# Token and key scores as eight-tile products, landmark rows on the partitions, landmark matrices 512 columns wide

## The chip, the cores and the metric

The kernel runs on one NeuronCore of a Trainium2 chip. TensorE multiplies matrices, VectorE, ScalarE and GpSimd work on elements, and SyncE issues the transfers. The metric is the device time of one execution in microseconds; the kernel before took 730.0 us (median of three runs, 729.05 to 730.16). In the profile TensorE is PE (its weight loads PEld), VectorE is DVE, ScalarE is ACT, GpSimd is POOL and SyncE is SP.

## The reference

Three layers in fp32: attention through landmarks, a gated MLP, and an MLP with a Mish activation. Four batches, eight heads, 576 tokens, head width 64, 32 landmarks of 18 tokens each.

```python
q_lm = q.reshape(B, H, 32, 18, D).mean(axis=3)
k_lm = k.reshape(B, H, 32, 18, D).mean(axis=3)
A  = sm(q, k_lm)         # token scores: softmax over the 32 landmarks, 576 x 32
Bm = sm(q_lm, k_lm)      # 32 x 32
C  = sm(q_lm, k)         # key scores: softmax over the 576 keys, 32 x 576
Z = Bm.T / (norm1(Bm) * norminf(Bm) + 1e-6)
for _ in range(6):
    Z = 2 * Z - Z @ Bm @ Z
attn = A @ Z @ C @ v                      # heads joined to x, 2304 x 512
x = ((x @ w1) * (x @ w2)) @ w3 @ w_out    # gated MLP, inner width 1024
h = x @ w_in                              # Mish MLP, inner width 2048
out = (h * tanh(softplus(h))) @ w_out2
```

sm(a, b) is the softmax of a @ b.T / 8 over the last axis.

## The kernel before

Everything after the softmaxes is linear up to the product a * b, so the kernel never forms attn. For each batch b it makes L = Z C v (kept transposed, LT, 256 landmark rows of all heads by 64) and from it the landmark matrices M = L w1 and L w2, one block of 128 columns of each (a slice s of eight) at a time. Then a = A M1 and b = A M2 (steps `xa` and `xb`), their product (`xm`) is the hidden h, and h times w3 @ w_out (made ahead by the steps `mm`) is the input y of the last layer (steps `y`). The Mish MLP follows with Strassen products (steps Z, O and their sums).

Products marked fp32 in the listing (scores, `mm`, M) run as two passes each and show as two matmuls in the profile. Products of split operands (high part and rest) run as three matmuls, lines 196 to 198.

Attention of one batch (function `attn`): `qs`, `ks` sum q and k over the 18 tokens of each landmark on DVE (L397). `bdq`, `bdk` place the sums of two heads in block-diagonal tiles (ACT or POOL, `blocks`). `as0` to `as2` make the token scores with tokens on the partitions: for 32 tokens at a time the stationary side is a block of q (128 rows, 32 columns) and the moving side one block-diagonal tile of 64 columns (L426). `amx`, `asb`, `aex`, `asm`, `aad`, `arc`, `amul` are the softmax over runs of 32 columns, in pieces of 512, 512 and (on 64 partitions) 256 columns; `atr` turns the result by PE transposes (L483), and `ahi`, `alo` split it into the tile AT. `cs0`, `cs1` make the key scores (L505, 288 columns, 64 stationary columns), `bs` the landmark scores (L588); `ctr`, `cv`, `lt` lead to LT, and `bp`, `nm`, `nu` are the iteration for Z. `m b s` makes one slice of M: eight fp32 products of 256 columns (L810) on eight tiles of the array, 64 rows by 32 columns each, into two PSUM banks, where each bank takes tiles of both row halves. `mh` (ACT) and `ml` (DVE, L225) split M into a slot of three, which `xa` and `xb` read.

Weights come as 512 KB tiles (`ld`), of which `da` (ACT or DVE) and `db` (DVE, L216) put the fp32 words together.

The order on all engines is written out in the table ORDER; `issue` runs the steps in that order, and each engine then works its instructions off in its own order, waiting for others by semaphores. The eight PSUM banks (pool `w`) are handed out in the same order. So an engine whose next instruction waits holds everything behind it.

Of the kernel before, what the change touches and what calls it, by code (L numbers as in the profile page):

```python
# [1481 lines left out]
```

## Time and profile before

| what | value |
|---|---|
| median of three runs | 730.0 us (729.05 to 730.16) |
| profiled execution | 729.66 us |
| its span, first to last instruction | 727.9 us |
| PE busy | 714.0 us, 98% |
| DVE busy | 410.2 us, 56% |
| ACT busy | 292.3 us, 40% |
| POOL busy | 15.2 us, 2% |
| mean granted PE clock, of full speed | 0.995 |

Shares are means over stages that differ. A line of a view that groups instructions gives their number, their busy time together (time in which at least one of them ran) and the mean duration of one; where matmuls run side by side or overlap, the busy time is far below number times duration. A line of the chain gives the start, the time and what ran.

### The profile page before, as it was taken

Reading aid. Unit: us, or ns where it says so; the run is one execution under the profiler, and the core shown is the slowest. Engines: PE = TensorE matmul, PEld = TensorE weight load, DVE = VectorE, ACT = ScalarE, POOL = GpSimd, SP = SyncE. Lnnn points to the kernel's source line nnn. Section 1 sums busy time; section 2 is a strip of 40 time slices with the busy share of each in tenths; the row PEclk is TensorE's granted clock in tenths of the full one; section 3 lists DMA queues with packets and bytes.
Section 4 is the critical chain, followed back from the end, with each engine's and each line's share of the span. In section 5 each row is a group of like instructions: output and inputs, shape, how many; then the busy total and the mean of one; then the engine's idle time right before and its main releaser. Section 6 shows DMA issues by size and latency. Waiting matters only on the chain.

```text
span 727.9 us, 13793 instructions
## 1 busy us (share of the span) xinstructions
PE 714.0 (98%) x5652; PEld 615.2 (85%) x5652; DVE 410.2 (56%) x896; ACT 292.3 (40%) x673; POOL 15.2 (2%) x37
## 2 busy tenths in 40 slices
PE   7799999999999999999999999999999999999997
PEld 4455899854999999999898898898898998898996
DVE  7889779846744734587565577733323553322322
ACT  2544446424534433465644445633222443222222
POOL 2111000000000000000000000000000000000000
PEclk9999999999999999999999999999999999999999
DMA  9876775343313053526554596687455545455402
GB/s 328 299 275 235 264 232 194 123 146 128 135 59 145 31 203 126 193 100 234 217 217 158 218 386 258 258 299 260 171 209 218 197 190 215 170 206 213 178 1 86
DMA packets 33918, 141.46 MB, mean 194 GB/s; under 512 B 3392, under 2 KB 3776, under 8 KB 30272
## 3 DMA queue, kind: packets, MB, share of 16 engines
q1 hardware_dynamic: 33712, 140.46, 52.4%
q8 instruction: 44, 0.72, 0.4%
q14 instruction: 18, 0.15, 0.1%
q10 hardware_dynamic: 144, 0.13, 0.1%
HBM read 110.69 MB, written 29.88 MB: 193 GB/s over the span
## 4 chain that ended last, share of the span: by engine, by line
PE 95%; DVE 2%; DMA 1%; issue 1%; ACT 0%; SPq 0%; ACTq 0%
PE ps L196 27%; PE ps L198 27%; PE ps L197 27%; PE ps L346 8%; PE ps L810 2%; PE ps L623 1%; DMA k<-in_kT_dram 1%; PE ps L564 1%; PE ps L505 1%; PE ps L483 1%; PE ps L426 1%; DVE sumk L397 1%; PE ps L543 1%; DVE sumq L397 0%; DVE mx L435 0%
## 5 line engine op out<-in xcount | busy, mean ns | idle before, releaser
L196 PE MATMUL ps<-hs,W 128*128 128x288 f32 (+1 forms) x298 | 92.5, 310 | 0.0
L197 PE MATMUL ps<-hs,W 128*128 128x288 f32 (+1 forms) x298 | 92.3, 310 | 0.0
L198 PE MATMUL ps<-hs,W 128*128 128x288 f32 (+1 forms) x298 | 92.2, 309 | 0.0
L1277 DVE TENSOR_TENSOR hsb<-ps,zt 128x384 f32<-128x384 f32 x72 | 39.8, 556 | 91.6 <-PE ps L198 91.6
L196 PE MATMUL ps<-AT,M 128*128 128x288 f32 x256 | 77.7, 303 | 0.0
L1273 ACT ACTIVATE hsb<-hsb 128x768 f32<-128x768 f32 (+1 forms) x48 | 32.8, 684 | 107.7 <-DVE hsb L1277 107.7
L198 PE MATMUL ps<-AT,M 128*128 128x288 f32 x256 | 75.5, 295 | 0.3 <-DVE M L225 0.3
L197 PE MATMUL ps<-AT,M 128*128 128x288 f32 x256 | 75.4, 294 | 0.0
L1277 DVE TENSOR_TENSOR zt<-ps,zt 128x384 f32<-128x384 f32 x48 | 26.7, 556 | 78.5 <-PE ps L198 74.6
L225 DVE TENSOR_TENSOR W<-hsb,W 128x384 fp32r<-128x384 f32 (+1 forms) x72 | 49.2, 686 | 18.1 <-ACT W L1274 18.1
L346 PE MATMUL ps<-wo,raw 128*128 128x512 f32 x128 | 59.4, 607 | 0.0
L196 PEld LDWEIGHTS ps<-hs,W 128*128 128x128 f32 x298 | 56.0, 188 | 2.1 <-issue 0.8
L198 PEld LDWEIGHTS ps<-hs,W 128*128 128x128 f32 x298 | 55.9, 188 | 1.8
L197 PEld LDWEIGHTS ps<-hs,W 128*128 128x128 f32 x298 | 56.1, 188 | 1.3
L196 PEld LDWEIGHTS ps<-AT,M 128*128 128x128 f32 x256 | 48.0, 188 | 3.4 <-issue 1.5
L197 PEld LDWEIGHTS ps<-AT,M 128*128 128x128 f32 x256 | 48.1, 188 | 0.5 <-issue 0.5
L198 PEld LDWEIGHTS ps<-AT,M 128*128 128x128 f32 x256 | 48.0, 188 | 0.5 <-DVE M L225 0.5
L220 ACT ACTIVATE a<-ps 128x288 f32<-128x288 f32 x64 | 25.5, 409 | 56.5 <-PE ps L198 49.9
L346 PEld LDWEIGHTS ps<-wo,raw 128*128 128x128 f32 x128 | 24.2, 199 | 24.9 <-issue 22.2
L204 ACT ACTIVATE top<-raw 128x512 f16<-128x512 bf16 x51 | 39.1, 786 | 14.7 <-DMA raw<-in_wts_dram 9.9
L848 DVE TENSOR_TENSOR h<-a,ps 128x288 f32<-128x288 f32 x64 | 27.9, 448 | 27.4 <-PE ps L198 24.8
L197 PE MATMUL ps<-yH,hs 128*128 128x384 f32 x120 | 40.2, 335 | 0.0
(191 smaller groups left out, 1597.6 us busy)
## 6 DMA issues: line engine op xcount, KB each, us to landing
raw<-in_wts_dram SPq DMA_DIRECT2D x88, 512.0 KB, 4.5
zw<-zd SPq DMA_DIRECT2D x8, 1792.0 KB, 7.5
hs<-zd SPq DMA_DIRECT2D x8, 1792.0 KB, 7.2
zd<-zw SPq DMA_DIRECT2D x4, 1792.0 KB, 7.1
zd<-hs SPq DMA_DIRECT2D x4, 1792.0 KB, 9.7
wy<-wod SPq DMA_DIRECT2D x12, 512.0 KB, 7.9
W<-wod SPq DMA_DIRECT2D x10, 512.0 KB, 7.3
q<-in_qT_dram SPq DMA_DIRECT2D x8, 576.0 KB, 7.5
```

The lines of the kernel that those rows point to most:

```text
L196: T.matmul(out=o, lhsT=lh, rhs=rh, start=first, stop=False, skip_group_check=partial)
L197: T.matmul(out=o, lhsT=lh, rhs=rl, start=False, stop=False, skip_group_check=partial)
L198: T.matmul(out=o, lhsT=ll, rhs=rh, start=False, stop=last, skip_group_check=partial)
L204: S.activation(o, i, ACTF.Copy)
L220: S.activation(o, x, ACTF.Copy)
L225: (G if e == "POOL" else V).tensor_tensor(o, x, f32(hi), op=ALU.subtract)
L346: T.matmul(out=got(f"acc{i}"), lhsT=f32(middle(got(f"w3{n}"))[:, o:o + 128]), rhs=WO0[j // 4][:, j % 4], start=j == 0, stop=j == 7)
L397: V.tensor_reduce(st["s" + x][:, r, :].rearrange("p a l -> p (a l)"), st[x][:, r, :].rearrange("p a (l t) -> p (a l) t", t=BLK_T), axis=AX ...
L810: T.matmul(out=got(f"p{c}{key}")[32 * i:32 * i + 32, 0:256], lhsT=LT[r, b, 2 * c + par, :], rhs=w12(f"w{bp}{s}{c}")[r, par * 256:par * 256 ...
L848: V.tensor_tensor(hslice(u, s), got("s" + key), got("b" + key)[:, 0:HALF], op=ALU.mult)
L1273: S.activation(e, src_, ACTF.Mish)
L1277: V.tensor_tensor(o, x, y, op=ALU.add)
```

## The change

It does these things:

- Token scores: the stationary side is now a landmark sum (64 rows of one head by 32 landmarks), the moving side 288 columns of q. Eight such products, four heads of each group g on 32 partitions each, go to eight tiles of the array (function `scores`). A batch needs two steps of eight products for the tokens (`as0`, `as1`, one for each half of the tokens) and two for the keys (`cs0`, `cs1`). The block-diagonal tiles and their copies go.
- Since softmax over landmarks now runs across partitions, DVE turns each 128x288 piece in blocks of 32x32 straight from PSUM (`at`), the softmax runs on two pieces of 576 columns, and a second block transpose of 576 columns on DVE (`atr`) takes the place of the PE transposes.
- The scale 1/8/18 moves into the exponentials. The landmark scores go to two banks, with one maximum and one subtraction for each.
- M is made for two slices at once: eight products of 512 columns into two full banks; `mt` hands out the slots of M apart from the product, so that a slot is claimed before the split and not before the product. The weight tiles of w1 and w2 are cut to match.
- ORDER is written anew from the first row to the last.

```diff
+        def lm_rows(g, i):
+            p, h2 = 2 * g + i // 2, (i ^ g) % 2
+            return p, slice(64 * h2, 64 * h2 + 64), (64 * h2, 32 * i)
+
+        def scores(key, lm, x, hf):
+            for i in range(4):
+                for g in range(2):
+                    p, r, at_ = lm_rows(g, i)
+                    T.matmul(out=mine(f"{key}{g}{hf}")[32 * i:32 * i + 32, 0:HALF], lhsT=st[lm][r, p, :],
+                             rhs=st[x][r, p, hf * HALF:(hf + 1) * HALF], start=True, stop=True, tile_position=at_)
...
-                            T.matmul(out=sc[r:r + 32, i, p * 64:p * 64 + 64], lhsT=st["q"][:, p, t0 + r:t0 + r + 32],
-                                     rhs=bdk[:, p, :], start=True, stop=True, tile_position=(0, r))
...
+        def a_turn(hf, g):
+            def f(e):
+                st["e", g] = mine(f"e{g}")
+                V.transpose(st["e", g][:, hf * HALF:(hf + 1) * HALF], mine(f"sc{g}{hf}")[:, 0:HALF])
             return f
...
-                        T.transpose(out=tp[:, c, i * 128:i * 128 + w],
-                                    in_=st["e", g][0:w, i, c * 128:(c + 1) * 128], identity=idn[0:w, 0:w])
...
+        def a_back(g):
+            def f(e):
+                V.transpose(mine(f"ea{g}"), st["e", g])
+            return f
...
-                        T.matmul(out=mine(f"cs{g}{hf}")[64 * pr:64 * pr + 64, 0:HALF], lhsT=bdq[:, 2 * g + pr, :],
-                                 rhs=st["k"][:, 2 * g + pr, hf * HALF:(hf + 1) * HALF], start=True, stop=True)
...
+        for hf in range(2):
+            add(f"as{hf}", "PE", [ks, "lq1"], a_scores(hf), (), {f"sc{g}{hf}": "w" for g in range(2)})
+        for hf in range(2):
+            for g in range(2):
+                add(f"at{hf}{g}", "DVE", [f"as{hf}"] + [f"at0{g}"] * hf, a_turn(hf, g), (), {} if hf else {f"e{g}": "e"}, [f"sc{g}{hf}"])
...
-            add(f"atr{g}", "PE", [f"amul{g}"], a_tr(g), (), {f"tp{g}": "w"}, [f"e{g}"])
+            add(f"atr{g}", "DVE", [f"amul{g}"], a_back(g), (), {f"ea{g}": "ea"}, [f"e{g}"])
...
-                    T.matmul(out=got(f"p{c}{key}")[32 * i:32 * i + 32, 0:256], lhsT=LT[r, b, 2 * c + par, :],
-                             rhs=w12(f"w{bp}{s}{c}")[r, par * 256:par * 256 + 256], start=True, stop=True,
+                    T.matmul(out=got(f"p{c}{key}")[32 * i:32 * i + 32], lhsT=LT[r, b, 2 * c + par, :],
+                             rhs=w12(f"w{bp}{s}{2 * c + par}")[r], start=True, stop=True,
                              tile_position=(64 * (h % 2), 32 * i))
...
+        for x in range(2):
+            n = f"{b} {2 * s + x}"
+            step(f"mt {n}", "none", vacated, lambda e: None, {f"M {n}": "M"})
+            for c in range(2):
+                step(f"mh{c} {n}", "ACT", [key, f"mt {n}"], ev(0, c, x))
+                step(f"ml{c} {n}", "DVE", [f"mh{c} {n}"], ev(1, c, x), (), [f"p{c}{key}"])
```

On DVE, at the token softmax of the first batch, the order was this (mx is the maximum, e the scores less the maximum, ps a PSUM bank):

```order
L435 TENSOR_REDUCE mx<-ps_80 128x16
L604 TENSOR_REDUCE bsm<-be 128x2
L397 TENSOR_REDUCE sumq<-q_71 128x64
L607 TENSOR_SCALAR bsm<-bsm 128x2
L514 TENSOR_REDUCE cmx<-ps_83 128x1
L442 TENSOR_TENSOR e_93<-ps_80,mx 128x512
```

It is now this, with the block transposes of batch 0 as they come from PSUM:

```order
L578 TENSOR_REDUCE bsm<-be 128x2
L420 STREAM_TRANSPOSE e_93<-ps_84 128x288
L498 TENSOR_SCALAR csm<-csm 128x1
L393 TENSOR_REDUCE sumk<-k_72 128x64
L581 TENSOR_SCALAR bsm<-bsm 128x2
L584 RECIPROCAL bsm<-bsm 128x2
L503 RECIPROCAL csm<-csm 128x1
L420 STREAM_TRANSPOSE e_94<-ps_83 128x288
L420 STREAM_TRANSPOSE e_94<-ps_77 128x288
```

The transposes stand where the first maximum stood; the first maximum now comes 24 rows behind the first transpose, and reads SBUF.

On PE, from the last product of LT to the first product of `xa` (AT and M are its operands, wo and raw those of an `mm` product, w and LT those of M), the order was this:

```order
L689 MATMUL ps_81<-py,cv 64x32 x2
L810 MATMUL ps_82<-w_875,LT 32x256
L810 MATMUL ps_78<-w_875,LT 32x256
...
L810 MATMUL ps_84<-w_875,LT 32x256
L810 MATMUL ps_81<-w_875,LT 32x256
...
L346 MATMUL ps_79<-wo_67,raw 128x512
L483 MATMUL ps_82<-idn,e_94 128x128 x4
L483 MATMUL ps_78<-idn,e_95 128x64 x2
L196 MATMUL ps_84<-AT_68,M 128x288
```

It is now this:

```order
L663 MATMUL ps_80<-py,cv 64x32 x2
L784 MATMUL ps_81<-w_669,LT 32x512
L784 MATMUL ps_84<-w_669,LT 32x512
...
L784 MATMUL ps_83<-w_669,LT 32x512
L784 MATMUL ps_80<-w_669,LT 32x512
...
L344 MATMUL ps_79<-wo_67,raw 128x512
L344 MATMUL ps_82<-wo_67,raw 128x512 x2
...
L344 MATMUL ps_78<-wo_67,raw 128x512
L344 MATMUL ps_77<-wo_67,raw 128x512
...
L194 MATMUL ps_81<-AT_68,M 128x288
```

Both batches' first M now holds two slices, eight `mm` products stand between it and `xa` where one stood, and the PE transposes there are gone. In the whole order 32 `mm` products of 64 stand ahead of the first `xa`, where 28 stood.

## Rows read from the trace of the kernel before

**Rows 1.** The page: busy time of all engines, then PE and DVE in slices.

```profile
PE 714.0 (98%) x5652; PEld 615.2 (85%) x5652; DVE 410.2 (56%) x896; ACT 292.3 (40%) x673; POOL 15.2 (2%) x37
...
PE   7799999999999999999999999999999999999997
...
DVE  7889779846744734587565577733323553322322
```

**Rows 2.** Windows: length, busy time (and count) of PE, PEld, DVE, ACT, POOL; clock; DMA.

```profile
0.00:10.00 10.00, 7.28 (x32) 2.95 (x32) 4.56 (x5) 1.88 (x4) 2.73 (x12) 1.00 0.78 281
10.00:71.60 61.60, 55.59 (x888) 31.56 (x888) 54.26 (x146) 27.83 (x80) 7.99 (x17) 0.94 0.80 285
71.60:145.00 73.40, 72.99 (x1044) 63.80 (x1043) 60.09 (x162) 37.39 (x101) 2.29 (x7) 1.00 0.60 206
145.00:330.00 185.00, 185.00 (x1696) 161.85 (x1694) 107.20 (x249) 78.99 (x206) 2.20 (x3) 1.00 0.37 131
330.00:727.90 397.90, 393.17 (x2004) 355.00 (x2002) 184.13 (x338) 146.25 (x286) 0.00 (x0) 1.00 0.54 206
```

**Rows 3.** Timeline, first 60 us: start, duration, engine, line; the last k lands.

```profile
9.98 1.35 DVE L397 TENSOR_REDUCE sumk<-k 128x64 f32<-128x1152 f32 x1 [0.17 <-DMA k<-in_kT_dram]
```

**Rows 4.** Timeline round the first product of xa.

```profile
69.99 1.59 DVE L225 TENSOR_TENSOR M<-ps,M 128x256 fp32r<-128x256 f32 x4 [0.53 <-ACT M L220]
...
71.62 0.40 PE L196 MATMUL ps<-AT,M 128*128 128x288 f32 x1
```

**Rows 5.** Waits of PE: who waited for whom, us in total, times, longest.

```profile
PE ps L564 <- issue: 2.8, 1, 2.8
```

**Rows 6.** Groups of PE by shape: count, busy us, mean ns, idle before.

```profile
L346 PE MATMUL ps<-wo,raw 128*128 128x512 f32 x128 | 59.4, 607 | 0.0
L810 PE MATMUL ps<-w,LT 64*32 64x256 f32 x512 | 17.6, 382 | 0.0
L426 PE MATMUL ps<-bdk,q 128*32 128x64 f32 x576 | 11.9, 231 | 1.2 <-issue 1.2
L505 PE MATMUL ps<-k,bdq 128*64 128x288 f32 x64 | 9.3, 416 | 1.4 <-DMA k<-in_kT_dram 1.2 <-ACT ce L524 0.2
```

**Rows 7.** Chain that ended last, 0 to 270 us: start, us, what.

```profile
68.89 1.03 PE ps L810 x32
...
112.39 0.36 PE ps L588 x8
...
135.38 2.09 PE ps L505 x16
...
145.23 9.45 PE ps L346 x22
...
155.31 1.02 PE ps L483 x8
...
159.27 1.03 PE ps L426 x64
160.31 0.69 PE ps L810 x16
...
166.96 0.57 PE ps L426 x16
...
168.86 0.27 PE ps L483 x2
```

**Rows 8.** Groups of DVE by shape.

```profile
L216 DVE SCALAR_TENSOR_TENSOR w<-raw,top 128x512 int32<-128x512 int32 x32 | 21.7, 683 | 3.3 <-ACT top L204 3.0
...
L435 DVE TENSOR_REDUCE mx<-ps 128x16 f32<-128x512 f32 x8 | 5.4, 680 | 0.0
...
L435 DVE TENSOR_REDUCE mx<-ps 64x8 f32<-64x256 f32 x4 | 1.6, 409 | 0.3 <-PE ps L426 0.3
...
L644 DVE STREAM_TRANSPOSE tr<-bc 128x128 f32<-128x128 f32 x4 | 1.2, 308 | 0.0
...
L618 DVE STREAM_TRANSPOSE bt<-bm 128x64 f32<-128x64 f32 x4 | 0.9, 235 | 0.0
```

More of the change, by code (lines that the diff above doesn't have):

```diff
@@ L311 @@
     pools["hs"] = [0, 1]
-    pools["e"] = [p0.tile([128, 2, 256], F32, name=f"e{i}") for i in range(3)]
+    pools["e"], pools["ea"] = ([p0.tile([128, S_LEN], F32, name=f"{x}{i}") for i in range(2)] for x in ("e", "ea"))
     pools["ce"] = [p0.tile([128, S_LEN], F32, name=f"ce{i}") for i in range(2)]
@@ L355, in add_w3_mm @@
                  (), [f"acc{i}"])
-    bds = [[p0.tile([128, NP, 2 * L], F32, name=f"bd{x}{i}") for x in "qk"] for i in range(2)]
     QKV = {"q": p0.tile([128, NP, S_LEN], F32, name="q"), "k": p0.tile([128, NP, S_LEN], F32, name="k")}
@@ L488, in f @@
             def f(e):
-                c0, n, w = chunks[g]
-                N = (n - 1) * 128 + w
-                s = slice(c0 * 128, c0 * 128 + N)
-                tp = st["at", g][:, :, 0:N]
                 if b not in AT:
@@ L495, in f @@
                 if i == 0:
-                    copy(e, AT[b][:, 0, :, s], tp)
+                    copy(e, AT[b][:, 0, g], mine(f"ea{g}"))
                 else:
-                    less(e, AT[b][:, 1, :, s], tp, AT[b][:, 0, :, s])
-            return f
-        def c_scores(g):
-            def f(e):
-                for hf in range(2):
-                    for pr in range(2):
-                        T.matmul(out=mine(f"cs{g}{hf}")[64 * pr:64 * pr + 64, 0:HALF], lhsT=bdq[:, 2 * g + pr, :],
-                                 rhs=st["k"][:, 2 * g + pr, hf * HALF:(hf + 1) * HALF], start=True, stop=True)
+                    less(e, AT[b][:, 1, g], mine(f"ea{g}"), AT[b][:, 0, g])
             return f
@@ L584, in b_scores, with b_max, b_sub @@
         def b_scores(e):
-            st["pb"] = small("pbm", 2, L)
-            for g in range(2):
-                for pr in range(2):
-                    T.matmul(out=st["pb"][64 * pr:64 * pr + 64, g, :], lhsT=bdq[:, 2 * g + pr, :],
-                             rhs=st["sk"][:, 2 * g + pr, :], start=True, stop=True)
-        def b_max(e):
-            st["bmx"] = sbt([128, 2], "bmx", 2)
-            V.tensor_reduce(st["bmx"], st["pb"], axis=AX.X, op=ALU.max)
-        def b_sub(e):
-            st["be"] = sbt([128, 2, L], "be", 2)
-            V.tensor_tensor(st["be"], st["pb"], st["bmx"].unsqueeze(2).to_broadcast([128, 2, L]), op=ALU.subtract)
+            st["pb"] = [mine(f"pb{g}")[:, 0:L] for g in range(2)]
+            for i in range(4):
+                for g in range(2):
+                    p, r, at_ = lm_rows(g, i)
+                    T.matmul(out=st["pb"][g][32 * i:32 * i + 32], lhsT=st["sq"][r, p, :], rhs=st["sk"][r, p, :],
+                             start=True, stop=True, tile_position=at_)
+        def b_max(g):
+            def f(e):
+                if g == 0:
+                    st["bmx"] = sbt([128, 2], "bmx", 2)
+                V.tensor_reduce(st["bmx"][:, g:g + 1], st["pb"][g], axis=AX.X, op=ALU.max)
+            return f
+        def b_sub(g):
+            def f(e):
+                if g == 0:
+                    st["be"] = sbt([128, 2, L], "be", 2)
+                V.tensor_scalar(st["be"][:, g, :], st["pb"][g], st["bmx"][:, g:g + 1], None, op0=ALU.subtract)
+            return f
         def b_exp(e):
-            S.activation(st["be"], st["be"], ACTF.Exp, scale=1.0 / BLK_T)
+            S.activation(st["be"], st["be"], ACTF.Exp, scale=scale / (BLK_T * BLK_T))
         def b_sum(e):
@@ L706, in attn @@
             add(f"lk{i}", "SP", [], load("k", i), [f"{x} {prior}" for x in ("ks4", "cs0", "cs1")])
-            add(f"lq{i}", "SP", [], load("q", i), [f"{x} {prior}" for x in ("qs4", "as0", "as1", "as2")])
+            add(f"lq{i}", "SP", [], load("q", i), [f"{x} {prior}" for x in ("qs4", "as0", "as1")])
         add("lv", "SP", [], load_v, old(1, "cv0", "cv1"))
         ks = sums("k")
-        both = ("ACT", "POOL")
-        bk, bq = [f"bdk{i}" for i in range(4)], [f"bdq{i}" for i in range(4)]
-        for i in range(4):
-            add(f"bdk{i}", both, [ks], blocks("k", bdk, i), old(2, "as0", "as1", "as2"))
         qs = sums("q")
-        for i in range(4):
-            add(f"bdq{i}", both, [qs], blocks("q", bdq, i), old(2, "cs0", "cs1", "bs"))
-        add("bs", "PE", bq + [ks], b_scores, (), {"pbm": "w"})
-        add("bmx", "DVE", ["bs"], b_max, old(2, "bsb"))
-        add("bsb", "DVE", ["bmx"], b_sub, old(2, "bml"), (), ["pbm"])
-        add("by", "ACT", ["bsb"], b_exp)
+        add("bs", "PE", [qs, ks], b_scores, (), {"pb0": "w", "pb1": "w"})
+        for g in range(2):
+            add(f"bmx{g}", "DVE", ["bs"], b_max(g), old(2, "bsb0", "bsb1"))
+        for g in range(2):
+            add(f"bsb{g}", "DVE", [f"bmx{g}"], b_sub(g), old(2, "bml"), (), [f"pb{g}"])
+        add("by", "ACT", ["bsb0", "bsb1"], b_exp)
         add("bsm", "DVE", ["by"], b_sum, old(2, "bml"))
@@ L742, in e_old @@
         def e_old(g, *names):
-            n = 3 * b + g - 3
-            return [f"{x}{n % 3} {n // 3}" for x in names] if n >= 0 else []
-        for g in range(3):
-            add(f"as{g}", "PE", bk + ["lq1"], a_scores(g), (), {f"sc{g}": "w"})
-            add(f"amx{g}", "DVE", [f"as{g}"], a_max(g), e_old(g, "asb"))
-            add(f"asb{g}", "DVE", [f"amx{g}"], a_sub(g), (), {f"e{g}": "e"}, [f"sc{g}"])
+            n = 2 * b + g - 3
+            return [f"{x}{n % 2} {n // 2}" for x in names] if n >= 0 else []
+        for hf in range(2):
+            add(f"as{hf}", "PE", [ks, "lq1"], a_scores(hf), (), {f"sc{g}{hf}": "w" for g in range(2)})
+        for hf in range(2):
+            for g in range(2):
+                add(f"at{hf}{g}", "DVE", [f"as{hf}"] + [f"at0{g}"] * hf, a_turn(hf, g), (), {} if hf else {f"e{g}": "e"}, [f"sc{g}{hf}"])
+        for g in range(2):
+            add(f"amx{g}", "DVE", [f"at0{g}", f"at1{g}"], a_max(g), e_old(g, "asb"))
+            add(f"asb{g}", "DVE", [f"amx{g}"], a_sub(g))
             add(f"aex{g}", "ACT", [f"asb{g}"], a_exp(g))
@@ L754, in attn @@
             add(f"amul{g}", ("POOL", "DVE"), [f"arc{g}"], a_mul(g))
-            add(f"atr{g}", "PE", [f"amul{g}"], a_tr(g), (), {f"tp{g}": "w"}, [f"e{g}"])
+            add(f"atr{g}", "DVE", [f"amul{g}"], a_back(g), (), {f"ea{g}": "ea"}, [f"e{g}"])
             add(f"ahi{g}", "ACT", [f"atr{g}"], a_out(g, 0), made)
-            add(f"alo{g}", "DVE", [f"ahi{g}"], a_out(g, 1), (), (), [f"tp{g}"])
+            add(f"alo{g}", "DVE", [f"ahi{g}"], a_out(g, 1), (), (), [f"ea{g}"])
         def c_old(g, *names):
@@ L761, in c_old @@
             return [f"{x}{n % 2} {n // 2}" for x in names] if n >= 0 else []
+        for hf in range(2):
+            add(f"cs{hf}", "PE", [qs, "lk1"], c_scores(hf), (), {f"cs{g}{hf}": "w" for g in range(2)})
         for g in range(2):
-            two = (f"cs{g}0", f"cs{g}1")
-            add(f"cs{g}", "PE", bq + ["lk1"], c_scores(g), (), {k: "w" for k in two})
             for i in range(3):
-                add(f"cm{i}{g}", "DVE", [f"cm{i - 1}{g}" if i else f"cs{g}"], c_max(g, i), c_old(g, "cex1"))
+                add(f"cm{i}{g}", "DVE", [f"cm{i - 1}{g}"] * (i > 0) + [f"cs{i}"] * (i < 2), c_max(g, i), c_old(g, "cex1"))
             for i in range(2):
@@ L821, in ev @@
             return f
-        step(key, "PE", [f"lte0 {b}", f"lte1 {b}", f"db w{bp}{s}0", f"db w{bp}{s}1"]
-             + vacated + chain("m", key), mm, {"p0" + key: "w", "p1" + key: "w", key: "M"},
-             [f"fw{bp}{s}0", f"fw{bp}{s}1"])
-        for c in range(2):
-            step(f"mh{c} {b} {s}", "ACT", [key], ev(0, c))
-            step(f"ml{c} {b} {s}", "DVE", [f"mh{c} {b} {s}"], ev(1, c), (), [f"p{c}{key}"])
+        step(key, "PE", [f"lte0 {b}", f"lte1 {b}"] + [f"db w{bp}{s}{x}" for x in range(4)]
+             + chain("m", key), mm, {"p0" + key: "w", "p1" + key: "w"}, [f"fw{bp}{s}{x}" for x in range(4)])
+        for x in range(2):
[4 more added lines that the diff above has]
+                step(f"ml{c} {n}", "DVE", [f"mh{c} {n}"], ev(1, c, x), (), [f"p{c}{key}"])
     def hslice(u, s):
@@ L851, in add_ab @@
             me = f"{x} {key}"
-            step(me, "PE", [f"ml0 {b} {s}", f"ml1 {b} {s}"] + [f"alo{g} {b}" for g in range(3)] + chain("x", me), ab(i),
-                 {"ab"[i] + key: "w"}, [f"m {b} {s}"])
+            step(me, "PE", [f"ml0 {b} {s}", f"ml1 {b} {s}"] + [f"alo{g} {b}" for g in range(2)] + chain("x", me), ab(i),
+                 {"ab"[i] + key: "w"}, [f"M {b} {s}"])
         step(f"xc {key}", "ACT", [f"xa {key}"], lambda e: copy(e, got("s" + key), got("a" + key)[:, 0:HALF]),
@@ L1110 @@
     vacated = [f"db {u}" for u in in_m] + [f"mm {u[2:]} {i}" for u in in_m if u[1] == "3" for i in range(4)]
-    for s in range(NS):
-        for c in range(2):
-            add_w12(0, s, c)
+    for s in range(NS // 2):
+        for x in range(4):
+            add_w12(0, s, x)
     for b in range(2, B):
         attn(b)
-    step("swap", "none", [f"{x} {b}" for b in range(B) for x in ("lte1", "lte0", "alo2", "cve1", "cv1")], swap)
+    step("swap", "none", [f"{x} {b}" for b in range(B) for x in ("lte1", "lte0", "alo0", "alo1", "cve1", "cv1")], swap)
     for bp in range(2):
         if bp:
-            for s in range(NS):
-                for c in range(2):
-                    add_w12(1, s, c)
+            for s in range(NS // 2):
+                for x in range(4):
+                    add_w12(1, s, x)
         for s in range(NS):
             for b in (2 * bp, 2 * bp + 1):
-                add_m(b, s)
+                if s % 2 == 0:
+                    add_m(b, s // 2)
             for b in (2 * bp, 2 * bp + 1):
@@ L1145 @@
     done_ab = [f"xb {b} 7 {h}" for b in (2, 3) for h in range(2)]
-    all_m = [f"m {b} 7" for b in (2, 3)]
+    all_m = [f"m {b} 3" for b in (2, 3)]
     y_in = [f"ye {u} {m}" for u in range(3) for m in range(4)]
@@ L1163, in made @@
         x = x_ops(n)
-        was = [last_read[MADE[s - 4]]] if s >= 4 else [f"db w1{6 + s // 2}{s % 2}"]
+        was = [last_read[MADE[s - 4]]] if s >= 4 else [f"db w13{s}"]
         step(x[0][0], "SP", was, x[0][2], {f"x {s}": "raw"} if s < 4 else {})
@@ L1395 @@
     G.memset(TOP, 0)
-    for x in bds:
-        for t in x:
-            G.memset(t, 0.0)
     ones = sbt([128, 512], "ones", 1, BF16)
@@ L1456 @@
         wts.append(halves(w3T[r0:r0 + 256, c0:c0 + 256]))
-    for s_ in range(8):
-        for c in range(2):
-            r, t = slice(256 * c, 256 * c + 256), slice(128 * s_, 128 * s_ + 128)
-            wts.append(halves(np.concatenate([w1[r, t], w2[r, t]], axis=1)))
+    for s_ in range(4):
+        for i in range(4):
+            r = slice(128 * i, 128 * i + 128)
+            wts.append(np.concatenate([w[r, t:t + 128] for t in (256 * s_, 256 * s_ + 128) for w in (w1, w2)], axis=1))
     for j in range(4):
```

77 lines of the change are left out of this document (24 added, 53 removed), and 265 rows, old and new, of the table ORDER.

## The prediction, made before the changed kernel ran

> **What bounds the kernel now.** I read the page first. PE is busy 714.0 of 727.9 us, and its row of slices stands at 9 from the third slice to the last but one; DVE is at 56% in all, but at 7 to 9 tenths in the first eight slices [rows 1]. So I cut the span where the first product of `xa` starts, at 71.62 us [rows 4], and asked for busy times by window [rows 2]. Two regimes stand side by side. From 71.6 us on PE idles 0.4 us up to 145 us, nothing from 145 to 330 us, and 4.7 us in the 397.9 us behind that: here the time is the sum of what PE has to do. Before 71.6 us PE idles 8.7 us, and what gates the first `xa` is DVE: from the landing of the last half of k [rows 3] to 71.6 us it is busy 54.3 of 61.6 us, and the last thing that `xa` waits for is the four `ml` of the first M, which end at 71.58 us on DVE [rows 4]. Of DVE's 7.3 idle us about 3 fall into one gap of 2.8 us in which PE waited for nothing the profile shows [rows 5]; the rest are short waits on ACT and PE. So: end = S + R, with S = 71.6 us the start of `xa`, set by DVE's queue, and R = 656.3 us, set by PE's work. The change takes work from PE and gives some to DVE, so it acts on R and S with opposite signs.
>
> **R, the work of PE behind the first xa.** The chain gives durations as they count, start to start [rows 7].
>
> - Token scores: a batch costs 1.03 + 1.03 + 0.57 = 2.63 us now. A new step is 8 products of 288 columns, in two passes 16 matmuls. The trace does not show it, but M has the same form with 256 columns: 32 matmuls take 1.03 us, 16 take 0.69 us, so 16 more cost 0.34 us and a start costs 0.35. Streaming grows by 288/256: 16 cost 0.38 + 0.35 = 0.73 us alone, 32 in a row 1.11 us. The two steps of a batch stand in a row nearly always, so 1.15 us. Saved 1.5 us for each batch; batches 2 and 3 come behind `xa`: 3.0 us. Bounds: all 32 as dear as the 128x64 products of 288 columns (2.09 us for 16, so 4.2 us, a loss of 1.5 a batch); below, no start at all, 0.77 us.
> - Key scores: 2.09 us for a batch now, 1.15 us then. Batch 2 is ahead of `xa` in both orders, so only batch 3 counts: 0.9 us.
> - PE transposes: 1.02 + 0.27 = 1.3 us a batch, gone: 2.6 us for batches 2 and 3.
> - M: 32 steps before, of which 30 behind `xa`; 512 matmuls are busy 17.6 us [rows 6], so 30 steps are 16.5 us. Then 14 steps of 16 matmuls of twice the columns. Each streams what a pair of old steps streamed, and a pair of old steps in a row cost 1.03 us [rows 7], so 14 x 1.03 = 14.4 us, and less where two stand in a row. I take 14.7 us, a saving of 1.8 (0 to 3).
> - `mm` products: 36 were behind the first `xa`, 32 are now. 22 matmuls take 9.45 us [rows 7], so a product of two is 0.86 us: 3.4 us less in R. This is no saving of work; PE does it where it idled.
> - Landmark scores: 8 matmuls in 0.36 us; 16 smaller ones on eight tiles then. I take nothing, within 0.4 us each way for a batch.
>
> Sum: 3.0 + 0.9 + 2.6 + 1.8 + 3.4 = 11.7 us off R. The savings of batch 0, all of batch 1, and batch 2's key scores fall in front of S, where PE idles anyway; I give them nothing. What hides them is DVE's queue, and if that cover were gone they would be worth about 8 us more.
>
> **S, the queue of DVE in front of the first xa.** I counted DVE's instructions in both orders up to the last `ml` that the first products wait for: 148 before, 156 now.
>
> - Added: 8 block transposes of 128x288 and 4 of 128x576. The trace has 64 columns in 235 ns and 128 in 308 ns [rows 8], so 1.14 ns for a column and 162 ns fixed: 490 ns and 819 ns, in all 3.9 + 3.3 = 7.2 us. Those rows read SBUF and the new ones read PSUM in part. Low end: as cheap as other operations by column (128x512 in 680 ns [rows 8], 1.33 with its fixed part), about 6.6 us; high end: the 128-column row for each 128 columns, 0.69 and 1.39 us, in all 11.1 us. I take the line through the two rows.
> - Added: two maxima and two subtractions of the landmark scores, estimate 0.7 us; three more joins `db` at 0.68 us [rows 8] = 2.1 us (they feed the four early `mm`); small ones 0.5 us.
> - Removed: softmax on four pieces of 576 columns in place of four of 512 (680 ns) and two of 256 (409 ns) [rows 8]: by columns 0.745 us each, over maximum, subtraction and sum 10.6 to 8.9, so 1.6 us; sums of rows and reciprocals 0.9; one multiplication that stood on DVE 0.4; two key sums of batch 2 at 1.34 us [rows 3] that now stand behind `xa`, 2.7.
>
> Net +4.9 us of durations; neighbours overlap by some 0.08 us, so eight more instructions give back 0.6: S moves by about +4.4 us. I add 0.8 us behind S. From the first `xa` to the 33rd `mm` product (145 us in the trace) the new order holds 60.7 us of DVE durations against 58.4 us of PE work; before, it was 72 against 73, and those 72 were 60.1 us busy [rows 2], so the 60.7 are some 50.6 us busy. At the 88% to which DVE packed its queue ahead of S that is 57.5 us: it just fits, and a few instructions of PE will find DVE late.
>
> DVE's new wait: `at` waits for `as`, and behind it stand weight joins that feed `mm`. It stands where `amx` stood, which waited for the same product; I cost it at nothing. PE's granted clock is 0.94 of full speed from 10 to 71.6 us [rows 2], so part of that stretch ran at the lower of its two levels, 1.2 GHz; with less to do ahead of S PE may stand there longer, which I also cost at nothing, since PE is not late there. ACT and POOL lose 32 small copies; neither is late anywhere before S.
>
> **Sum.** 727.9 - 11.7 + 4.4 + 0.8 = 721.4 us of span. The profiled execution took 729.66 us, 1.8 us more than its span: 723.2 us. It lies 0.3 us under the median of 730.0 us, so I say 723 us, with 719.5 to 727 as this case's own range.
>
> **Two rules that speak against it.** M already puts tiles of both row halves into one bank, and 512 matmuls are busy 17.6 us, 34 ns each, where one of 512 columns on the whole array takes 430 ns, so 215 ns for 256 columns [rows 6, 7]: more than six run at once. The Trainium skill (TensorEngine Tiling (Array Packing), Restrictions and Gotchas, Gotcha 1: PSUM Pressure) says that different row tiles cannot write the same PSUM bank at the same time; by that the scores would go in two rounds of four. This case's trace disagrees, at 34 ns for a matmul where two rounds would need 54; it stays as a rival with a small chance. That DVE stood at 54.3 of 61.6 us ahead of `xa` is the row for the other [rows 2]: the same page (Performance Considerations, PSUM Bottleneck) says that tiling speeds TensorE but not the emptying of PSUM, which may then be the bound. The trace agrees that DVE is the bound there; its price is rival 3.
>
> **Rivals.**
>
> 1. DVE has slack. The PE gap [rows 5] has no work behind it that needs it; if it does not come again, DVE packs its queue closer, S moves by +1 instead of +4.4, nothing is late behind it: 719 us, 715 to 719.5. With S unmoved it is 718 us. For it: ahead of S PE has some 48 us of work in 75 (32 `mm` at 0.86 us are 27.5 of them), so nothing there waits for PE long. Against: the gap belongs to nothing that the change touches.
> 2. Rounds of four. A score matmul of 288 columns would need 54 x 288/256 = 61 ns in place of 38: the 96 behind `xa` cost 2.2 us more, and the ten steps of 16 in front of S hold DVE up by up to 0.37 us each, 3.7 us. 723 + 5.9 = 729 us, no change. Rows 6 speak against it.
> 3. Slower: DVE becomes the bound of the attention stage. Transposes at their high end add 3.9 us in front of S, and the 8.8 us are packed at 88%: S + 10. Behind S the other twelve add 3.9 too, and at the 82% that DVE showed from 71.6 to 145 us [rows 2] its work there lasts 61.7 us against PE's 58.4: 3.3 us late. 727.9 - 11.7 + 10 + 3.9 + 3.3 + 1.8 = 735 us, 731 to 737. It decides the sign once S passes 83 us. Against it: high-end transposes contradict the two rows.
>
> **How the numbers follow.** Forecast 0.52; rival 1 0.24; rival 2 0.08; rival 3 0.13; something outside (the orders of the later stages, which are new too, with PE's work there the same) 0.03. Range 715 to 731 us: rival 1 down to its lower end, rival 2 whole, the mild part of rival 3; about 0.1 is left out above and 0.08 below. What a measurement can tell from no change is 0.2%, 1.5 us. Faster than 728.5 us: forecast, rival 1, part of rival 2, 0.79; within: 0.08; slower than 731.5 us: 0.13.
>
> **What would show it.** PE has some 5000 instructions in place of 5652. The score products are busy about 10 us in place of 21 (L426 and L505), M about 15 in place of 17.6. STREAM_TRANSPOSE of 288 columns near 0.49 us, of 576 near 0.82; 0.69 and 1.39 point to rival 3. The first L194 starts near 76 us; at 73 rival 1, past 83 rival 3. Behind it PE idles under 2 us up to 150 us. Wrong would be: L405 at 50 ns a matmul or more in busy time, the first `xa` earlier than 70 us, or several us of PE idling behind DVE in the slices of 75 to 150 us.

## The result, and the profile after

The changed kernel took 718.1 us (median of four runs, 717.5 to 719.3) against 730.1 us for the kernel before in the same session: a ratio of 0.984, 95% interval 0.982 to 0.986. It is faster by 12 us, inside the range, and 5 us under the forecast of 723. It also lies below the likeliest case's own range (719.5 to 727): the time is that of rival 1. The profiled execution took 719.34 us with a span of 717.5 us; the other three had spans of 715.8 to 716.8 us at a slightly higher mean granted clock (0.989 to 0.993, against 0.988).

The page of the changed kernel: busy time with share and count, then PE, DVE and PE's granted clock in 40 slices. It answers to [rows 1].

```profile
PE 702.5 (98%) x5004; PEld 597.5 (83%) x5004; DVE 419.1 (58%) x904; ACT 287.3 (40%) x649; POOL 11.2 (2%) x13
...
PE   7799999999999999999999999999999999999997
...
DVE  6999879768545555975756766543223553322322
...
PEclk8799999999999999999999999999999999999999
```

PE lost 11.5 us of busy time and 648 instructions. DVE gained 8.9 us and stands at 9 tenths in slices 2 to 4, where it stood at 8, 8 and 9. The clock row starts with 8 and 7: PE ran part of the first 36 us at the lower of its two levels.

The windows of the changed kernel, cut as in [rows 2] but at its own first `xa`, 73.07 us (length, busy time and count of PE, PEld, DVE, ACT, POOL, clock, DMA).

```profile
10.00:73.07 63.07, 56.52 (x723) 26.42 (x723) 60.00 (x156) 29.54 (x76) 5.09 (x4) 0.86 0.84 299
73.07:145.00 71.93, 71.90 (x776) 59.16 (x775) 60.39 (x149) 34.85 (x91) 2.31 (x2) 1.00 0.58 198
145.00:330.00 185.00, 184.81 (x1568) 165.52 (x1567) 117.38 (x274) 85.15 (x222) 2.65 (x2) 1.00 0.38 135
330.00:717.50 387.50, 382.60 (x1922) 343.95 (x1920) 176.82 (x324) 136.42 (x261) 0.00 (x0) 1.00 0.55 208
```

R is 717.5 - 73.07 = 644.4 us, where it was 656.3: 11.9 us less, against the 11.7 of the sum. S moved by 1.5 us, from 71.62 to 73.07, where the sum had 4.4. In front of `xa` DVE is busy 60.0 of 63.1 us, 95%, where it was 54.3 of 61.6. Behind it PE idles 0.03 us up to 145 us and 0.2 us up to 330 us; the 0.8 us that I added for late DVE work did not come.

The timeline of the changed kernel round the first `xa` (start, us, engine, what); it answers to [rows 4].

```profile
66.49 7.14 PE L344 MATMUL ps<-wo,raw 128*128 128x512 f32 x16
...
70.80 1.62 DVE L223 TENSOR_TENSOR M<-ps,M 128x256 fp32r<-128x256 f32 x4
...
73.07 0.70 PE L194 MATMUL ps<-AT,M 128*128 128x288 f32 x1
```

Before, `xa` started 0.04 us after the last `ml`. Now the four `ml` end at 72.42 us, and `xa` comes only when PE has worked off its eight `mm`, with no idle time. PE has become the later of the two here, by 0.65 us.

PE's groups behind the first `xa`, first of the kernel before (from 71.62 us), then of the changed one (from 73.07 us): count, busy us, mean ns, idle before.

```profile
L346 PE MATMUL ps<-wo,raw 128*128 128x512 f32 x72 | 32.5, 598 | 0.0
...
L810 PE MATMUL ps<-w,LT 64*32 64x256 f32 x480 | 16.5, 382 | 0.0
...
L426 PE MATMUL ps<-bdk,q 128*32 128x64 f32 x288 | 5.3, 220 | 0.0
...
L483 PE MATMUL ps<-idn,e 128*128 128x128 f32 (+1 forms) x22 | 3.1, 268 | 0.0
...
L505 PE MATMUL ps<-k,bdq 128*64 128x288 f32 x16 | 2.2, 412 | 0.0
```

```profile
L344 PE MATMUL ps<-wo,raw 128*128 128x512 f32 x66 | 30.1, 599 | 0.0
...
L784 PE MATMUL ps<-w,LT 64*32 64x512 f32 x224 | 13.9, 596 | 0.0
...
L405 PE MATMUL ps<-q,sumk 64*32 64x288 f32 x64 | 2.6, 409 | 0.0
L405 PE MATMUL ps<-k,sumq 64*32 64x288 f32 x32 | 1.8, 415 | 0.0
```

Where the 11.9 us went: `mm` 2.4 (its last two matmuls ahead of `xa` still run across the cut), M 2.6, token scores 2.7, PE transposes 3.1, key scores 0.4, and 0.4 on the landmark scores (0.9 to 0.5). That is 11.6. Not all of it is work saved. The `mm` part now runs ahead of `xa`. So do two more slices of M: 480 matmuls of 256 columns are 30 slices at 0.55 us, 224 of 512 are 28 slices at 0.50, so 1.1 us of M's 2.6 is moved and 1.5 saved.

The new operations in the whole program, PE's and then DVE's groups (same columns).

```profile
L784 PE MATMUL ps<-w,LT 64*32 64x512 f32 x256 | 15.8, 596 | 0.0
L405 PE MATMUL ps<-k,sumq 64*32 64x288 f32 x128 | 9.2, 479 | 3.2 <-DVE sumq L393 1.1 <-DMA k<-in_kT_dram 1.0 <-ACT top L202 0.8
...
L405 PE MATMUL ps<-q,sumk 64*32 64x288 f32 x128 | 7.2, 476 | 0.4 <-ACT ce L491 0.4
```

```profile
L420 DVE STREAM_TRANSPOSE e<-ps 128x288 f32<-128x288 f32 x16 | 6.9, 459 | 0.0
...
L463 DVE STREAM_TRANSPOSE ea<-e 128x576 f32<-128x576 f32 x8 | 6.0, 755 | 0.0
```

The transposes cost 459 and 755 ns, a little under the line through the two rows (490 and 819). The scores are busy 16.4 us, not about 10: the 96 matmuls behind `xa` take 4.4 us, 46 ns each, and the 160 ahead of it 12.0 us, 75 ns each. Of these 160, 64 run between 12 and 24 us, where the granted clock is 0.50, and are busy 6.8 us.

### The profile page after: what moved, and what is told of

Read it like the earlier page. It is cut to its first block, busy times and chain, and to the rows that moved or that the text cites. A ratio compares the mean times of both kernels' runs of the same rounds, so it can differ in the third digit from the quotient of the medians.

```text
span 717.5 us, 12433 instructions
## 1 busy us (share of the span) xinstructions
PE 702.5 (98%) x5004; PEld 597.5 (83%) x5004; DVE 419.1 (58%) x904; ACT 287.3 (40%) x649; POOL 11.2 (2%) x13
## 4 chain that ended last, share of the span: by engine, by line
PE 94%; DMA 2%; DVE 2%; ACT 1%; issue 0%; SPq 0%; ACTq 0%; DVEq 0%
PE ps L194 27%; PE ps L195 27%; PE ps L196 27%; PE ps L344 7%; PE ps L784 2%; DMA raw<-in_wts_dram 2%; PE ps L405 1%; PE ps L597 1%; DMA q<-in_qT_dram 1%; PE ps L531 1%; PE ps L510 0%; DVE e L420 0%; DVE cmx L481 0%; DVE mx L426 0%; DVE ea L463 0%
## 5 line engine op out<-in xcount | busy, mean ns | idle before, releaser
L202 ACT ACTIVATE top<-raw 128x512 f16<-128x512 bf16 x48 | 37.3, 785 | 8.8 <-DMA raw<-in_wts_dram 6.2
L195 PE MATMUL ps<-yH,zw 128*128 128x384 f32 x120 | 40.3, 336 | 0.1
```

The lines of the kernel that those rows point to most:

```text
L195: T.matmul(out=o, lhsT=lh, rhs=rl, start=False, stop=False, skip_group_check=partial)
L202: S.activation(o, i, ACTF.Copy)
```

## The experiments

Two theories at first: A, PE's own work, unbroken from about 31 us on, sets the first `xa`; B, as predicted, DVE's queue does. Each kernel is the changed one with one edit. In each session the kernel before took 729.9 to 730.7 us.

**The old scores (e1).** The products of L405 are replaced.

```
-            return lambda e: scores("sc", "sk", "q", hf)
+            return lambda e: old_a(hf)    # 36 products 128x32 by 56 to 72 columns
-            return lambda e: scores("cs", "sq", "k", hf)
+            return lambda e: old_c(hf)    # 4 products 128x64 by 288 columns
```

> The changed kernel, but its token and key scores are made by products of the shape of before: 36 products of 128x32 by about 64 columns for a half of the tokens, four of 128x64 by 288 columns for a half of the keys (the operands are not the right ones, so the scores are not the reference's; all else stays). Prices from the traces: a batch of token scores 2.6 us in place of 1.1, of key scores 2.1 in place of 1.2. Theory A (PE, not DVE, holds everything up from about 31 us on, where its last long wait ends, so each product behind that counts in full): token scores of batches 1 to 3 and key scores of batches 2 and 3 come back, 3 x 1.5 + 2 x 0.9 = +6.3 us on the changed kernel's 718.1, 724.4. Theory B (the prediction's: DVE's queue sets the first xa, only what lies behind it counts): batches 2 and 3 of the tokens and 3 of the keys, +3.9, 722.0, with the first xa unmoved at 73. Theory C (the gain comes from the new order and not from the products): under +1.5.

727.4 us, ratio 0.996 (0.995 to 0.997): 9.2 us more, so the products, with what comes along with them, carry most of the gain, and theory C falls. It is more than A or B gave. The timeline of e1 shows why.

```profile
143.34 1.21 PE L412 MATMUL ps<-q 128*32 128x58 f32 x72
144.48 0.42 PE L611 MATMUL ps<-py 32*32 32x64 f32 x16
144.83 1.07 PE L412 MATMUL ps<-q 128*32 128x58 f32 x61
149.32 0.58 PE L412 MATMUL ps<-q 128*32 128x72 f32 x11 [3.41 <-issue]
```

In the middle of the products PE stands still for 3.4 us, and the releaser is "issue": the profile shows nothing that it waited for. The kernel before had such a gap of 2.8 us [rows 5]. The gap in e1 costs more than its length. Behind it PE's granted clock is 0.71 from 150 to 155 us, and the eight matmuls of `mm` there take longer than the 3.71 us of the next eight:

```profile
150.40 4.92 PE L344 MATMUL ps<-wo,raw 128*128 128x512 f32 x8
```

R in e1 is 725.7 - 73.27 = 652.4 us, 8.0 more than in the changed kernel: 3.4 for the gap, 1.2 for the slower `mm`, and 3.4 left for the products, which were priced at 3.9.

The DMA queues of e1 from 146 to 148 us (packets, MB, share of 16 engines):

```profile
q1 hardware_dynamic: 304, 0.64, 97.2%
q8 instruction: 1, 0.02, 2.8%
```

Data transfers fill the engines, and between them one transfer of instructions lands. The first `xa` came at 73.27 us, against 71.6 to 71.8 in e2, e4, e10 and e11, which leave the work ahead of it alone but for e2's halved first M: 1.6 us for the products ahead of it.

**The same with fewer instructions (e9).** Only batch 3's token products differ from e1.

```
-            return lambda e: old_a(hf)
+            return lambda e: long_a(hf) if b > 2 else old_a(hf)    # 8 products by 288 columns
```

> As the kernel with products of the old shape (e1), but batch 3's token scores are made by 8 products of 128x32 by 288 columns for a half in place of 36 by about 64: the same columns through the same four column groups, with 32 matmuls in place of 144 for the batch (operands not the right ones, so the scores are not the reference's). In e1 PE stood still for 3.4 us in these products, with nothing in the profile that it waited for; a 16 KB transfer of an instruction queue lies in 146 to 148 us, inside that gap. Theory I (PE ran out of instructions, after some 220 short matmuls in 4.1 us): the gap is gone, and the products are some 0.7 us shorter: 727.4 - 3.4 - 0.7 = 723.3. If the gap has another cause (a bank, a wait that the profile doesn't show, where it stands in the order): a gap of 3 us or more stays near 146 us, 726.5 to 727.4.

722.5 us, ratio 0.990 (0.988 to 0.991): 4.9 us less than e1. The timeline of e9 at the same place:

```profile
143.99 1.18 PE L425 MATMUL ps<-q 128*32 128x288 f32 x16
145.10 0.43 PE L617 MATMUL ps<-py 32*32 32x64 f32 x16
145.46 1.18 PE L425 MATMUL ps<-q 128*32 128x288 f32 x16
146.56 0.43 PE L617 MATMUL ps<-py 32*32 32x64 f32 x16
```

No gap, and the eight matmuls of `mm` behind it (at 146.92 us) take 3.71 us again. R is 721.0 - 73.92 = 647.1 us, 5.3 less than in e1: 3.4 for the gap, 1.2 for the clock behind it, the rest for the shorter products. The same columns go through the same column groups, in 32 matmuls where there were 144: the gap in e1 goes when the number of matmuls falls. The transfers alone do not make it. In e9, too, data fill the DMA engines from 145 to 149 us and one transfer of instructions lands among them, and PE is busy without a break from 145 to 150 us:

```profile
q1 hardware_dynamic: 590, 1.52, 100.4%
q8 instruction: 1, 0.02, 1.5%
```

That PE ran out of instructions is the reading nearest at hand, but no view shows PE's supply of them, so it is argued. That the gap of the kernel before is of that kind is not shown directly (e1 did not bring it back at its place, 28 us). It looks the same: it stands among 40 matmuls of 64 columns, and an instruction transfer lands in it while data take all DMA engines.

**M in halves of 256 columns (e2).**

```
-                for c in range(2):
+            for x in (slice(0, 256), slice(256, 512)):   # the same eight products for each half
```

> The changed kernel, but each product of M with 512 columns is issued as two of 256, so that M has its 512 matmuls of before. By the groups M was busy 16.5 us behind the first xa before and 13.9 after. If the width is what saved that, M is busy 17.5 us again and the time is +2.0 to +2.6 us, 720.1 to 720.7. If M's saving only came from the order (steps standing in a row), M stays under 16.3 us and the time within 0.7 of 718.1.

719.2 us, ratio 0.984 (0.982 to 0.986): no change. M's group of e2 behind the first `xa`:

```profile
L785 PE MATMUL ps<-w,LT 64*32 64x256 f32 x448 | 13.9, 379 | 0.0
```

Twice the matmuls, the same 13.9 us. So the wider product saves nothing. What is left is that two slices are made in one go: 0.50 us a slice in place of 0.55, which is 1.5 of M's 2.6 us (the other 1.1 is moved ahead of `xa`). That is the expectation's second reading; its time, within 0.7 us of 718.1, was missed by 0.4, and lies inside the spread of the changed kernel's own four runs.

**The block transposes twice, ahead (e3) and behind (e4).**

```
-                V.transpose(mine(f"ea{g}"), st["e", g])
+                for _ in range(2 if b < 2 else 1):    # e4: b > 1; likewise in a_turn
+                    V.transpose(mine(f"ea{g}"), st["e", g])
```

> The changed kernel with the block transposes of batches 0 and 1 on DVE issued twice, the same result twice: 8 x 0.46 + 4 x 0.76 = 6.7 us of durations more in front of the first xa, some 5.7 us of queue when neighbours overlap by 0.08. Theory B (DVE's queue sets S): the first xa moves from 73.1 to 78.8, time +5.7, 723.8. Theory A (PE sets it, the ml that xa needs are done 1.5 us earlier): +4.2, 722.3. Theory D (DVE has real slack there): under +1.

> The changed kernel with the block transposes of batches 2 and 3 issued twice: the same 6.7 us of DVE, but behind the first xa, where PE was busy 71.87 of 71.9 us and DVE 60.4. Theories A and B: PE's work alone sets the time there, within 0.7 us of 718.1. The third rival of the prediction (DVE becomes the bound of the attention stage): +3 to +6, with PE waiting for DVE between 75 and 200 us.

e3: 727.0 us, ratio 0.995 (0.993 to 0.997), +8.9. e4: 722.7 us, ratio 0.990 (0.988 to 0.993), +4.6. All theories missed e3. In e4 theories A and B missed, and the reading by rival 3 came true (+3 to +6, with PE waiting for DVE). The first `xa` of e3, and PE's longest waits in it (us in total, times, longest):

```profile
81.19 0.70 PE L194 MATMUL ps<-AT,M 128*128 128x288 f32 x1
```

```profile
PE ps L599 <- DVE bt L594: 4.6, 1, 4.6
PE ps L599 <- DVE py L656: 3.4, 2, 3.2
```

R is 725.6 - 81.19 = 644.4 us, exactly as without the edit; all of it falls on S, which moves by 8.1 us (from 73.07 us) for 6.7 us of DVE durations. DVE has no slack there. More than the durations is lost; PE's waits for the short steps of the iteration for Z (`bt`, `py`) are the ones that grew. In e4 PE's waits stand where batch 3's softmax is (timeline of e4):

```profile
147.65 0.30 PE L514 MATMUL ps<-idn,ce 128*64 128x128 f32 x1 [0.28 <-DVE e L421]
148.53 0.33 PE L599 MATMUL ps<-bt 32*32 32x32 f32 x16 [0.58 <-DVE e L421]
149.72 0.42 PE L599 MATMUL ps<-py 32*32 32x64 f32 x16 [0.86 <-DVE py L656]
```

R rises to 720.5 - 71.61 = 648.9 us, by 4.5. PE's idle time behind `xa` grows by 2.2 us of that, 1.7 in these three waits; where the rest goes is not settled. DVE was not idle cover behind `xa` either: the mechanism of rival 3 is real, the changed kernel stays just short of it.

**Four `mm` products behind `xa` (e5).**

```
-mm 3 3,mm 7 1,mm 7 0,da w010@ACT,db w010,mm 7 3, ... mm 7 2,xa 0 0 0,xb 0 0 0,
+mm 3 3,da w010@ACT,db w010, ... xa 0 0 0,xb 0 0 0,mm 7 1,mm 7 0,mm 7 3,mm 7 2,
```

> The changed kernel with four of the mm products (3.4 us of PE) moved in ORDER from in front of the first xa to behind the first xa and xb. Theory B (DVE's queue sets the first xa): xa stays at 71.6 to 73.1, the 3.4 us are added behind, 721.5. Theory A (PE sets it, DVE is ready 1.5 us earlier): xa moves forward by 1.5, the time is +1.9, 720.0. If DVE has even more slack, xa moves by 3.4 and the time stays within 0.7 of 718.1.

722.5 us, ratio 0.989 (0.988 to 0.991): +4.4. PE in e5:

```profile
65.42 3.71 PE L344 MATMUL ps<-wo,raw 128*128 128x512 f32 x8
70.95 0.37 PE L194 MATMUL ps<-AT,M 128*128 128x288 f32 x1 [1.82 <-ACT M L218]
...
72.91 4.96 PE L344 MATMUL ps<-wo,raw 128*128 128x512 f32 x8
```

With 3.4 us less to do PE starts `xa` only 0.7 us earlier than the 71.6 of undisturbed runs, because it waits 1.8 us for M's split. After that idle time PE's granted clock over 71.6 to 100 us is 0.94, and eight matmuls of `mm` take 4.96 us where they took 3.71. So A and B are both half right: PE's work and the way to M (ACT and DVE) end within 0.7 us of each other.

**Matmuls on ones where PE waits (e6).**

```
+        for _ in range(n):    # 4 before bp 0, 5 before mm 4 0, 4 before nm0 0
+            T.matmul(out=got(key), lhsT=SPARE[0][:, 0:128], rhs=SPARE[0], start=True, stop=True)
```

> The changed kernel with 13 matmuls on ones (128x512) put on PE where it waits in batch 0: four before the first product on bt (a wait of 2.0 us), five before the first mm (1.3 us), four before the first product on py (1.0 us). They read and write nothing that is used. In the changed kernel's profile the granted clock was 0.5 from 12 to 24 us and again round 33 us, in the runs with the first xa at 71.6 only the first time. Theory A (PE's chain from about 31 us sets the first xa): with the second fall gone, xa comes at 71.6 always, the time is 717.5 with a narrower spread, at best 716 if the first fall goes too. Theory B (DVE's queue sets it): no change, 718.1 with xa at 73. The matmuls cost time (up to +1.5) if what follows them was ready sooner than the waits of one profile say.

718.6 us, ratio 0.984 (0.982 to 0.986): no change. The granted clock from 10 to 30 us rises from 0.66 to 0.83 and is 1.00 from 30 to 50 us; `xa` comes at 71.90. So the first fall costs nothing. The second fall does cost, in the execution that has it. Here are the changed kernel, then e10, whose edit lies behind the first `xa`: the window from 30 to 36 us, the string of `mm` that begins there, and the next `py` step on DVE.

```profile
30.00:36.00 6.00, 5.35 (x77) 2.96 (x78) 5.83 (x22) 4.38 (x11) 0.00 (x0) 0.72 0.93 324
32.44 4.24 PE L344 MATMUL ps<-wo,raw 128*128 128x512 f32 x6
37.11 0.29 DVE L654 SCALAR_TENSOR_TENSOR py<-py,ps 128x128 f32<-128x128 f32 x1 [1.18 <-PE ps L597]
```

```profile
30.00:36.00 6.00, 6.00 (x123) 3.45 (x129) 5.90 (x24) 4.87 (x13) 0.00 (x0) 0.97 0.85 286
32.19 2.85 PE L344 MATMUL ps<-wo,raw 128*128 128x512 f32 x6
35.76 0.28 DVE L654 SCALAR_TENSOR_TENSOR py<-py,ps 128x128 f32<-128x128 f32 x1
```

Up to there DVE's queues lie within 0.1 us of each other. At the lower clock the same six matmuls take 1.4 us longer, DVE waits for the `py` product that stands behind them, and both engines stay 1.4 us late up to `xa` (73.07 against 71.71). What made the clock fall is not shown: e8 has the same wait of PE, 1.0 us for `py`, at 30 us and a clock of 1.00 from 30 to 36 us. Whether this fall makes the spread from run to run is not shown either: e6 was to narrow it, and its four runs still lie between 717.6 and 719.5 us.

**DVE work to POOL, and an order for it (e7, e8, e12).**

```
-                V.tensor_tensor(by_token(g), by_token(g), ... op=ALU.subtract)
+                (G if e == "POOL" else V).tensor_tensor(by_token(g), by_token(g), ... op=ALU.subtract)
```

> The changed kernel with the subtraction of the maximum of the token softmax on POOL in place of DVE for batches 0 and 1 (possible now that the scores lie in SBUF): DVE loses four operations of 128x576 at 0.75 us in front of xa, 3.0 us; POOL, which takes 1.26 us for the multiplication of that size, adds some 0.5 us of latency to each. The doubled early transposes cost 8.9 us for 6.7 us of DVE, so theory F (in front of xa PE waits for DVE early, from 16 to 31 us, and every us of DVE there is worth about one): -2 to -4, 714 to 716. Theory A (PE's own chain from 31 us on sets xa): within 0.7 of 718.1.

> The same, and the rest of AT of batch 0 (two differences of 128x576, 0.74 us each) on POOL too: DVE loses 4.5 us in front of xa. Theory F: -3 to -5, 713 to 715. Theory A: within 0.7 of 718.1; a loss if POOL ends AT later than xa needs it.

> The subtraction on POOL for batches 0 and 1 (e7), and in ORDER: the first wo's join on DVE stands right behind w34's (it waited 5.8 us in DVE's queue), the second mm product stands in front of the first product on py, where PE waited 1.0 us, and batch 0's maxima, subtractions and exponentials of the token softmax come behind py. DVE has 3.0 us of slack from e7 to pay for it. Theory A (PE's unbroken work from 31 us on sets xa): PE starts it 1.3 us (wo) + 1.0 us (py) earlier, xa at 69.5 to 70.5 in place of 71.5, 715.5 to 717. If M's split is the end that holds (ready at 70.95 in e5): at most -0.6, 717.4.

e7 718.0 us, ratio 0.983 (0.981 to 0.985), `xa` at 71.54; e8 718.9, 0.984 (0.983 to 0.986), at 72.54; e12 718.5, 0.984 (0.983 to 0.986), at 72.05. None beats the changed kernel. Theory F falls: 3.0 us off DVE leave `xa` where it was, though 6.7 us on it move it by 8.1. In e12 PE's wait for `wo` (1.3 us in e7) and the one of 1.0 us for `py` are gone, but it idles 7.3 us from 10 to 71.6 us, where e7 idles 6.8: its wait for `bt` is 3.1 us where e7's is 2.0, and there are new short ones. Why the early waits trade places like this is not settled.

**Token products four times, and with one row half for each bank (e10, e11).**

```
-            return lambda e: scores("sc", "sk", "q", hf)
+            return lambda e: [scores("sc", "sk", "q", hf) for _ in range(4 if b > 1 else 1)]
-                    p, r, at_ = lm_rows(g, i)    # e11
+                    p, r, at_ = (i, slice(64 * g, 64 * g + 64), (64 * g, 32 * i)) if key == "sc" and b > 1 else lm_rows(g, i)
```

> The changed kernel with the token score products of batches 2 and 3 issued four times, the same result each time: 6 x 32 matmuls more behind the first xa, 1.13 us for 32 in the chain. PE's work alone sets the time there: +6.0 to +6.8, 724.1 to 724.9, with R (from the first xa to the end) 644.4 + 6.4. If the products were covered by something: under +2. If tiles went in two rounds of four (1.95 us for 32): +11.7. Theory I (instructions run short): an idle stretch of PE without a releaser in batch 2 or 3 on top of that.

> The same with other tiles: each PSUM bank takes the four products of one row half (rows 0 to 63 or 64 to 127 of q and of the sums) in place of two of each (other heads, so the scores of batches 2 and 3 are not the reference's). If tiles of different row halves cannot write one bank at the same time, this is faster: down to half the time for the 256 products of these batches, 3 to 4 us less than the kernel before it. If the bank doesn't matter: the same within 0.7 us.

e10 724.1 us, ratio 0.992 (0.990 to 0.994); e11 723.9, 0.992 (0.990 to 0.994). The score group, the same line in e10 and in e11:

```profile
L405 PE MATMUL ps<-q,sumk 64*32 64x288 f32 x320 | 11.7, 405 | 1.2 <-ACT ce L491 0.9 <-DVE be L570 0.3
```

The two agree to the digit, and behind `xa` both are busy 8.4 us for 256 matmuls: which row half a bank takes doesn't matter. R in e10 is 721.9 - 71.71 = 650.2 us, 5.8 more for 192 matmuls, 30 ns each: behind `xa` a product costs what PE needs for it. No gap of the kind of e1 appeared.

## Why the prediction was right, and where not

- **R, right: 11.9 us against 11.7.** Token scores 2.7 (I had 3.0), PE transposes 3.1 (2.6), M 2.6 (1.8), key scores 0.4 (0.9), landmark scores 0.4 (0), `mm` 2.4 (3.4; without the two matmuls that run across the cut it is 3.4). The errors cancel, which is luck. e10 confirms the principle, that PE's work behind `xa` counts in full. M's term was reasoned rightly, as pairs of steps in a row; e2 shows that this and not the width is the saving, and 1.1 us of the term are the two slices moved ahead of `xa`.
- **S, mis-sized: +1.5 us against +4.4.** The time came inside the range because rival 1 stood in it; the forecast's own S did not come. The step that failed is the one from durations to time: the sum adds DVE's new durations to S as if the idle time of DVE's queue ahead of `xa`, 7.3 us, would stay. The durations were not overrated: DVE's busy time from 10 us to `xa` grew by 5.7 us, where the sum had 4.9. But the idle time fell from 7.3 to 3.1 us, and to 1.6 in e10 (60.0 us busy of 61.6). DVE's longer waits there, of the kernel before and then all of the changed one (us in total, times, longest):

```profile
DVE py L680 <- PE ps L623: 3.8, 2, 3.0
DVE raw L216 <- ACT top L204: 0.7, 1, 0.7
DVE M L225 <- ACT M L220: 0.5, 1, 0.5
```

```profile
DVE py L654 <- PE ps L597: 1.4, 2, 1.2
DVE bsm L578 <- ACT be L574: 0.3, 1, 0.3
```

The 3.0 us are DVE's share of the gap [rows 5]. Without them the old queue would have been busy 54.3 of 58.7 us, 93% (an estimate), where the new one runs at 95%, and at 97% in e10. So the gap is the larger part, and the waits for ACT, 2.1 us in all before and 0.3 now, are the other. Both are gone in the new order; which of its parts did it is not shown. In executions without the second fall of the clock S hardly moved: 71.6 to 71.8 us in e2, e4, e10 and e11, and an estimated 715.8 - 644.4 = 71.4 us in the fastest run of the changed kernel.

- **The gap, rival 1's ground.** I gave it 0.24, "against: the gap belongs to nothing that the change touches". e1 and e9 speak against that sentence: such a gap comes with many short matmuls and goes when their number falls, and the change took 648 matmuls off PE. For the gap of the kernel before this is argued, not shown; no run put the old products back in the old order with fewer matmuls.
- **DVE's slack, wrong for rival 1 too.** Rival 1 took DVE to have room. e3 and e4 show none, ahead of `xa` or behind it: 6.7 us more cost 8.9 and 4.6. That the new order "just fits" behind `xa` was right: up to the 33rd `mm` product (73.07 to 132.32 us) DVE is busy 50.7 of 59.3 us, where I had 50.6 of 58.4, and the 0.8 us of stalls were 0.2.
- **PE ahead of `xa`, wrong.** "PE is not late there" and a lower clock "at nothing": PE's `mm` now end later than `ml`, and the second fall of the clock is worth 1.4 us (73.07 against 71.71), through DVE's wait for PE at 37 us. A cost of nothing held for the first fall alone (e6).
- **Scores, wrong in size:** 16.4 us busy against 10, that is 64 ns a matmul, past the 50 ns that I had named as a sign of being wrong. Of the 256 matmuls 160 run ahead of `xa`, 64 of them at a granted clock of 0.50. Little of it counts there; behind `xa` it is 46 ns.
- **Two slips in the sum for S.** The low end of the transposes is 8 x 0.38 + 4 x 0.77 = 6.1 us, not 6.6; they measured 6.7. And 4.9 less 0.6 is 4.3, not 4.4. Neither changes the forecast.
- **Rounds of four (rival 2), refuted.** The Trainium skill (TensorEngine Tiling (Array Packing), Gotcha 1: PSUM Pressure) says that different row tiles cannot access one PSUM bank at the same time; e11 keeps them apart and gains nothing, 11.7 us either way.
